# Attention, routing and two expert layers in one kernel: whole-chunk loads, masks before scans, two sets of one-hots, and the weight decoding's last steps inside the last expert

## The chip, the core and the metric

The kernel runs on one core of a Trainium2 chip. The metric is device time in microseconds (us); the time before is the median of three runs.

## The reference

The reference chains three stages. The first is a gated linear attention over 4 batches, 8 heads, 768 steps and a head width of 48. The second is a mixture of 8 experts with the two best per token, and the third a dense gated layer over all 3072 tokens.

```python
for t in range(S):
    state = alpha[:, :, t, :, None] * state + np.einsum('bhd,bhe->bhde', k[:, :, t], v[:, :, t])
    y[:, :, t] = np.einsum('bhd,bhde->bhe', q[:, :, t], state)
...
noisy_logits = x @ w_gate + np.log1p(np.exp(x @ w_noise)) * noise
top2 = np.argpartition(-noisy_logits, 2, axis=1)[:, :2]
...
h = np.maximum(x[mask] @ w1[e], 0.0)
out[mask] += top2_w[mask, k, None] * (h @ w2[e])
...
a = x @ w_a
b = x @ w_b
return (a * b @ w_out).astype(np.float32)
```

The weights of the third stage arrive as 64-bit floats; the kernel turns them into 32-bit floats on the chip.

## The kernel before, in words

The order of the work is written out by hand: each engine runs its instructions in the order in which the program issues them, and generators (`tick` for the routing, `bg` for the decoding) put side work between units of the main work. TensorE carries the main work.

**Attention.** Tokens go in 24 chunks of 128 (6 per batch). A chunk's q, k and alpha of all heads stand in one tile `ring[i % 6]` of 128 rows by 1536 columns: one head of each pair in rows 0 to 47, the other in rows 64 to 111. `load_qka` (L457) brings it. Chunks 0 to 5 come as full 128-row images from `qka0`, with zeros and ones in the 16 rows behind each half; later ones as two transfers of 48 rows from `qka1`, since the padding rows are then already in the tile. `prep(i)` (L496) runs two scans on VectorE (L503 into D, L507 into A) that make the products of decays, and GpSimd multiplies k and q by them (L505, L508, L511). The loop at L637 handles chunk i: it issues the loads of chunk i+5, then `prep(i+3)`, then transposes and gate inputs on TensorE, one `tick()`, the state's part of the output (`inter`, L549), the scores of chunk i+1 (`sc_unit`, L533) with the causal masks on VectorE (L538, into pm), then `intra` (L557), the gate products (L617), the state's update (`u_unit` L584, `s_unit` L599 and L600), each with further ticks. Scores use PSUM banks 2 and 3, so the scores of a chunk wait until the masks of the chunk before have read them.

**Routing.** `route(g)` (L216) is a generator for 14 and then 10 chunks; it ranks experts and places tokens with many small VectorE operations, partly on GpSimd. After the second group `lists()` (L356) makes the gather lists: for five chunks at a time VectorE writes one-hots `at` (L369), `eqk` (L369) and `bt` (L375), TensorE multiplies them into a list (L382) and VectorE adds it up (L383, into idx at the end). `at`, `eqk` and `bt` have one buffer each, and between making a set and multiplying it the generator yields four times. `weights()` (L386) follows.

**Experts.** Each expert has `up_unit`s (nine products per unit and column block, L682 to L684, read by L699 on ScalarE and L700 on VectorE; four PSUM banks in turn) and `down_unit`s (24 products). Gathers of the rows of the next expert go from GpSimd's queue (L415), and `x_unit` transposes them (L423, L425, L426). Expert 0 runs in two parts; behind the second part's up units the program flushes the routing (`while side: tick()`, L911) and issues the seven gathers of expert 1.

**Decoding.** `decode(c)` (L836) turns piece c of 36 of the 64-bit weights into floats in five steps, one per `bg()`: a load; ScalarE L845 and L846 with VectorE L847; VectorE L850 and L851; ScalarE L853 with GpSimd L854 and L855; VectorE L857 and a store. When expert 6 is done, `while decs: bg()` (L954) issues all steps that are left, ahead of expert 7's first up unit, so that the pool `dec` can be released and the tile EX take its place.

Of the kernel before, what the change touches and what calls it, by code (L numbers as in the profile page):

```python
# [8 lines left out]
F32R = mybir.dt.float32r  # L9
# [11 lines left out]
NT = B * NCH  # L21
# [39 lines left out]
@with_exitstack  # L61
def moe_kernel(ctx: ExitStack, tc, qka0, qka1, afirst, v, wgn, noise, w1, w2, w3, out):
    nc = tc.nc
# [10 lines left out]
    def bank(i):  # L74
        return tl(psum, [128, 512], F32, f"bank{i}")
# [78 lines left out]
    rows = sctx.enter_context(tc.tile_pool(name="rows", bufs=7))  # L154
    rt = sctx.enter_context(tc.tile_pool(name="rt", bufs=1))

# [59 lines left out]
    def route(g):  # L216
# [90 lines left out]
        if half:  # L307
# [3 lines left out]
            else:  # L311
# [10 lines left out]
        yield  # L322
        eq, bt = (tl(rt, [128, HOT, 2, E * NJ], F16, x).rearrange("p a k w -> p (a k w)")[:, :n * NJ]
                  .rearrange("p (a w) -> p a w", a=n) for x in ("eqk", "bt"))
# [7 lines left out]
        for j0 in range(0, n, m):  # L332
            at = tl(rt, [128, HOT, 2, 128], F16, "at").rearrange("p a k w -> p (a k) w")[:, :m]
            nc.vector.tensor_tensor(at, lane[:, None, :].to_broadcast([128, m, 128]),
                                    pf[:, j0:j0 + m, None].to_broadcast([128, m, 128]), op=ALU.is_equal)
            for _ in range(LAG):
                yield
            pl = spot(1, NJ)
            for j in range(m):
                nc.tensor.matmul(pl, at[:, j], bt[:, j0 + j], start=j == 0, stop=j == m - 1)  # L340
            acc = lacc[:, mine]
            nc.vector.tensor_tensor(idx0[:, mine] if j0 + m == n else acc, pl[:, mine], acc, op=ALU.add)
# [13 lines left out]
    def lists():  # L356

        pi, ki, pf, kf = (tl(rt, [128, NT, 2], dt, x) for x, dt in (("ei", I32), ("ri", I32), ("rf", F32), ("e1", F32)))
        nc.vector.tensor_scalar(pi, slot, 127, None, op0=ALU.bitwise_and)
        nc.vector.tensor_scalar(ki, slot, 7, None, op0=ALU.logical_shift_right)  # L360
        nc.vector.tensor_copy(pf, pi)
        nc.vector.tensor_copy(kf, ki)
        for j0 in range(0, NT, HOT):
            m = min(HOT, NT - j0)
            js = slice(j0, j0 + m)
            at, eq, bt = (tl(rt, [128, HOT, 2, w_], F16, x) for x, w_ in (("at", 128), ("eqk", E * NJ), ("bt", E * NJ)))
            for out_, src, val in ((at, lane, pf), (eq, keys, kf)):
                w_ = src.shape[-1]
                nc.vector.tensor_tensor(out_[:, :m].rearrange("p a k w -> p (a k) w"),  # L369
                                        src[:, None, :].to_broadcast([128, 2 * m, w_]),  # L370
                                        val[:, js].rearrange("p a k -> p (a k)")[:, :, None]
                                        .to_broadcast([128, 2 * m, w_]), op=ALU.is_equal)
                yield
            for k in range(2):
                nc.vector.tensor_tensor(bt[:, :m, k], eq[:, :m, k],  # L375
                                        token[:, js, None].to_broadcast([128, m, E * NJ]), op=ALU.mult)
            for _ in range(LAG + 1):
                yield
            pl = spot(1, E * NJ)
            for j in range(m):  # L380
                for k in range(2):
                    nc.tensor.matmul(pl, at[:, j, k], bt[:, j, k], start=j + k == 0, stop=j == m - 1 and k == 1)  # L382
            nc.vector.tensor_tensor(idx if j0 + m == NT else lacc, pl, lacc, op=ALU.add)  # L383
        yield
# [62 lines left out]
    with ExitStack() as actx:  # L447
# [9 lines left out]
        def load_qka(i):  # L457

            t = ring[i % RING]
            if i < 2:  # L460
                for c in (slice(1024, 1536), slice(512, 1024), slice(0, 512)):
                    nc.sync.dma_start(t[:, c], qka0[i, :, c])
            elif i < RING:
                nc.sync.dma_start(t[:, :1536], qka0[i])
            else:
                for h in range(2):
                    nc.sync.dma_start(t[64 * h:64 * h + 48, :1536], qka1[i - RING, 48 * h:48 * h + 48])

# [168 lines left out]
        for i in range(NT):  # L637
            if i + 5 < NT:
                load_qka(i + 5)
                load_v(i + 5)  # L640
            if i + 3 < NT:
                prep(i + 3)
            if i + 1 < NT:
# [5 lines left out]
            if i + 1 < NT:  # L649
                sc_unit(i + 1)  # L650
            else:
                x_unit(0, 0, bank(2))
                x_unit(0, 1, bank(3))
            tick()
            intra(i)
# [255 lines left out]
    while side:  # L911
        tick()
    for q in range(NJ):
        gather(1, q)
# [13 lines left out]
    for e in range(1, E - 1):  # L928
# [14 lines left out]
        for j in range(NJ):  # L943
# [9 lines left out]
            bg()  # L953
    while decs:  # L954
        bg()
    dec.release()
    epool = sctx.enter_context(tc.tile_pool(name="epool", bufs=1))
    EX = tl(epool, [128, (NF2 - 2) * 768], F32R, "EX")
    e = E - 1
    for f in range(NF1):  # L960
# [5 lines left out]
        if f >= NF1 - 4:  # L966
            load_more()
    tail = up_tail(e)
    next(tail)
# [177 lines left out]
```

## Time and profile before

| | us |
|---|---|
| median of 3 runs | 1097.96 |
| lowest, highest run | 1096.56, 1103.16 |
| the profiled execution | 1102.63 |
| its span on the core | 1100.8 |

The profile is of one execution, 4.7 us above the median. Its span leaves 1.8 us around it, and its mean granted TensorE clock is 0.984 of full speed. Times within it count from the span's start. In a row of the timeline stand the start, the time that the group took, engine, line, operation, operands and count; in brackets the engine's idle time before it and what ended that.

### The profile page before, as it was taken

What the parts mean: (1) busy time and instruction counts of PE and PEld (TensorE: products, weight loads), DVE (VectorE), ACT (ScalarE), POOL (GpSimd) and SP (SyncE); (2) the same over time, 40 slices, a digit from 0 to 9 for tenths busy, and PEclk for the clock granted to TensorE, in tenths of its full rate; (3) what the DMA queues carried; (4) which work ended last, traced back from release to release, by engine and by line L of the source; (5) the groups of instructions that cost most, each with busy time, mean ns of one, the idle gap of its engine ahead of it and who ended that gap; (6) DMA issues with size and microseconds to landing.
All of it is one profiled execution on the core that took longest, in us unless ns stands there. A gap on an engine that the chain in (4) does not pass through costs nothing.

```text
span 1100.8 us, 19103 instructions
## 1 busy us (share of the span) xinstructions
PE 1060.8 (96%) x7504; PEld 1026.1 (93%) x7504; DVE 467.2 (42%) x860; ACT 421.1 (38%) x929; POOL 405.4 (37%) x437
## 2 busy tenths in 40 slices
PE   7999899799999999999989999999999999999997
PEld 5888779799999999999978999999999999999997
DVE  8867846553342535353521453232323141414130
ACT  2435342354444555455542553222323232313131
POOL 5657631484654757575752553010101010100000
PEclk9989899999999999999998999999999999999999
DMA  8998322363544545544532552010101111010000
GB/s 284 217 199 192 97 73 83 111 217 100 168 134 140 163 155 171 173 162 152 176 122 79 165 164 70 22 44 22 37 29 29 37 30 37 22 37 1 22 1 24
DMA packets 59330, 114.57 MB, mean 104 GB/s; under 512 B 8144, under 2 KB 43776, under 8 KB 59232
## 3 DMA queue, kind: packets, MB, share of 16 engines
q1 hardware_dynamic: 52688, 93.49, 28.9%
q0 software_dynamic: 6544, 19.77, 6.0%
q8 instruction: 63, 1.03, 0.4%
q14 instruction: 35, 0.29, 0.1%
HBM read 86.38 MB, written 26.84 MB: 103 GB/s over the span
## 4 chain that ended last, share of the span: by engine, by line
PE 87%; DVE 5%; issue 3%; POOL 2%; ACT 1%; DMA 1%; another core or an unknown queue 0%; SPq 0%; POOLq 0%; ACTq 0%; DVEq 0%
PE bank L682 25%; PE bank L684 25%; PE bank L683 25%; PE bank L423 2%; PE bank L533 2%; PE bank L557 2%; PE bank L549 1%; PE bank L525 1%; PE bank L584 1%; DVE D L503 1%; DVE pm L538 1%; DVE A L507 1%; PE bank L494 1%; DMA wst<-w3f 1%; POOL rf L855 1%
## 5 line engine op out<-in xcount | busy, mean ns | idle before, releaser
L682 PE MATMUL bank<-X,W 128*128 128x384 f32 (+2 forms) x768 | 261.0, 340 | 4.6 <-DVE HB L700 3.9
L683 PE MATMUL bank<-X,W 128*128 128x384 f32 (+2 forms) x768 | 259.6, 338 | 0.6 <-DVE X L426 0.6
L684 PE MATMUL bank<-X,W 128*128 128x384 f32 (+2 forms) x768 | 259.6, 338 | 0.0
L114 POOL TENSOR_TENSOR W<-wst,W 128x384 fp32r<-128x384 f32 x136 | 139.0, 1028 | 145.4 <-ACT W L113 133.9
L880 POOL DMA_INDIRECT row<-y,row x48 | 46.3, 964 | 295.1 <-DVE row L888 186.2
L682 PEld LDWEIGHTS bank<-X,W 128*128 128x128 f32 x768 | 145.5, 189 | 7.7 <-DVE HB L700 4.6
L683 PEld LDWEIGHTS bank<-X,W 128*128 128x128 f32 x768 | 145.6, 190 | 2.8 <-DVE X L426 0.9
L684 PEld LDWEIGHTS bank<-X,W 128*128 128x128 f32 x768 | 145.3, 189 | 2.2
L682 PE MATMUL bank<-W,HB 128*128 128x384 f32 x416 | 145.6, 350 | 0.1
L684 PE MATMUL bank<-W,HB 128*128 128x384 f32 x416 | 140.9, 339 | 0.0
L683 PE MATMUL bank<-W,HB 128*128 128x384 f32 x416 | 140.7, 338 | 0.0
L1000 DVE TENSOR_TENSOR p<-bank,a 128x384 f32<-128x384 f32 x96 | 53.5, 557 | 166.7 <-PE bank L684 166.4
L426 DVE TENSOR_TENSOR X<-bank,X 128x384 fp32r<-128x384 f32 (+1 forms) x80 | 42.8, 538 | 182.7 <-ACT X L425 181.0
L1001 ACT ACTIVATE HB<-p 128x384 fp32r<-128x384 f32 x96 | 50.5, 526 | 155.7 <-DVE p L1000 152.1
L700 DVE SCALAR_TENSOR_TENSOR HB<-bank,HB 128x384 fp32r<-128x384 f32 (+2 forms) x128 | 71.2, 563 | 88.5 <-ACT HB L699 78.4
L699 ACT ACTIVATE HB<-bank 128x384 fp32r<-128x384 f32 (+2 forms) x128 | 63.4, 497 | 94.7 <-PE bank L684 82.1
L682 PE MATMUL bank<-EX,HB 128*128 128x384 f32 x240 | 82.1, 342 | 0.0
L683 PE MATMUL bank<-EX,HB 128*128 128x384 f32 x240 | 80.4, 335 | 0.0
L684 PE MATMUL bank<-EX,HB 128*128 128x384 f32 x240 | 80.3, 335 | 0.0
L682 PEld LDWEIGHTS bank<-W,HB 128*128 128x128 f32 x416 | 78.1, 188 | 0.8 <-ACT HB L699 0.4
L683 PEld LDWEIGHTS bank<-W,HB 128*128 128x128 f32 x416 | 78.3, 188 | 0.1
L684 PEld LDWEIGHTS bank<-W,HB 128*128 128x128 f32 x416 | 78.0, 188 | 0.2 <-DVE HB L700 0.2
(217 smaller groups left out, 1792.8 us busy)
## 6 DMA issues: line engine op xcount, KB each, us to landing
wst<-w SPq DMA_DIRECT2D x128, 192.0 KB
wd<-w SPq DMA_DIRECT2D x36, 384.0 KB
ring<-qka SPq DMA_DIRECT2D x36, 288.0 KB
y<-o SPq DMA_DIRECT2D x49, 192.0 KB
w3f<-u SPq DMA_DIRECT2D x36, 192.0 KB
wst<-w3f SPq DMA_DIRECT2D x36, 192.0 KB
v<-v SPq DMA_DIRECT2D x12, 384.0 KB
xd<-x SPq DMA_DIRECT2D x12, 384.0 KB
```

Source lines behind the costliest of these rows:

```text
L114: eng.tensor_tensor(l, raw, h.bitcast(F32), op=ALU.subtract)
L423: nc.tensor.transpose(pt[:, k * 128:k * 128 + m], t[:m, k * 128:k * 128 + 128], ident[:m, :m])
L426: nc.vector.tensor_tensor(l, ptv, h.bitcast(F32), op=ALU.subtract)
L533: nc.tensor.matmul(pb[h][:, p * 128:p * 128 + 128], part(i, h, NP + p), part(i, h, p), start=True, stop=True)
L682: nc.tensor.matmul(ps, ah, bh, start=first, stop=False)
L683: nc.tensor.matmul(ps, ah, bl, start=False, stop=False)
L684: nc.tensor.matmul(ps, al, bh, start=False, stop=last)
L699: nc.scalar.activation(Hh[:, f, s], pu, AF.Relu)
L700: nc.vector.scalar_tensor_tensor(Hl[:, f, s], pu, 0.0, Hh[:, f, s].bitcast(F32), op0=ALU.max, op1=ALU.subtract)
L880: nc.gpsimd.indirect_dma_start(out=t, out_offset=None, in_=src, in_offset=bass.IndirectOffsetOnAxis(ap=row[:, i, k:k + 1], axis=0))
L1000: nc.vector.tensor_tensor(p, ps[1], a, op=ALU.mult)
L1001: nc.scalar.activation(Ph[:, f], p, AF.Copy)
```

## The change

- **Loads.** The host pads all 24 chunks to 128 rows, in one array `qka`. From chunk 2 on each chunk is one transfer of 128 rows by 1536; the two transfers of 48 rows are gone (18 chunks, 18 fewer issues, 196,608 bytes more per chunk).
- **Masks ahead of scans.** `prep(i + 3)` moves in the loop from behind the loads to behind the scores of chunk i+1, so its scans stand behind that chunk's masks on VectorE.
- **One-hots.** `at`, `eqk` and `bt` have two buffers. `lists()` makes set j+1 before it multiplies set j, and yields three times per set where it yielded six times. The pool `rt` is taken from the other side of SBUF and released behind the flush of the routing.
- **Last decoding steps.** The up units of expert 7 each end with a `bg()`; the flush of the decoding, the release of `dec` and the allocation of EX stand behind them.

```diff
-            elif i < RING:
-                nc.sync.dma_start(t[:, :1536], qka0[i])
             else:
-                for h in range(2):
-                    nc.sync.dma_start(t[64 * h:64 * h + 48, :1536], qka1[i - RING, 48 * h:48 * h + 48])
+                nc.sync.dma_start(t[:, :1536], qka[i])
...
-            if i + 3 < NT:
-                prep(i + 3)
             if i + 1 < NT:
                 t_unit(i + 1)
...
                 x_unit(0, 1, bank(3))
+            if i + 3 < NT:
+                prep(i + 3)
             tick()
             intra(i)
...
+        yield from make(0)
+        for j0 in range(0, NT, HOT):
+            if j0 + HOT < NT:
+                yield from make(j0 + HOT)
+            else:
+                for _ in range(LAG):
+                    yield
+            m, at, bt = hot.pop(j0)
             pl = spot(1, E * NJ)
             for j in range(m):
                 for k in range(2):
                     nc.tensor.matmul(pl, at[:, j, k], bt[:, j, k], start=j + k == 0, stop=j == m - 1 and k == 1)
+            yield
             nc.vector.tensor_tensor(idx if j0 + m == NT else lacc, pl, lacc, op=ALU.add)
...
-    while decs:
-        bg()
-    dec.release()
-    epool = sctx.enter_context(tc.tile_pool(name="epool", bufs=1))
-    EX = tl(epool, [128, (NF2 - 2) * 768], F32R, "EX")
     e = E - 1
     for f in range(NF1):
         up_unit(e, f, [(0, CAPA)])
...
             load_more()
+        bg()
+    while decs:
+        bg()
+    dec.release()
+    epool = sctx.enter_context(tc.tile_pool(name="epool", bufs=1))
+    EX = tl(epool, [128, (NF2 - 2) * 768], F32R, "EX")
```

`make(j0)` holds the one-hot instructions of a set, unchanged, with the new buffers and two yields.

VectorE at the head of the attention loop, before; D and A are the scans, pm the masks, ss the state's update:

```order
L503 SCALAR_TENSOR_TENSOR D_235<-ring_35_129,bank_30_124 128x512
L506 RECIPROCAL bank_31_125<-D_235 128x4
L507 SCALAR_TENSOR_TENSOR A_236<-ring_35_129,bank_31_125 128x512
L503 SCALAR_TENSOR_TENSOR D_245<-ring_36_130,bank_30_124 128x512
L506 RECIPROCAL bank_31_125<-D_245 128x4
L507 SCALAR_TENSOR_TENSOR A_246<-ring_36_130,bank_31_125 128x512
L538 TENSOR_TENSOR pm_71_272<-bank_69_262,causal_72 128x512
L538 TENSOR_TENSOR pm_72_274<-bank_70_263,causal_72 128x512
L599 TENSOR_TENSOR ss_305<-bank_29_117,sc_233 128x192
```

The same place on VectorE now (L503 is L512, L538 is L547, L599 is L608):

```order
L512 SCALAR_TENSOR_TENSOR D_235<-ring_35_129,bank_30_124 128x512
L515 RECIPROCAL bank_31_125<-D_235 128x4
L516 SCALAR_TENSOR_TENSOR A_236<-ring_35_129,bank_31_125 128x512
L547 TENSOR_TENSOR pm_68_263<-bank_66_253,causal_72 128x512
L547 TENSOR_TENSOR pm_69_265<-bank_67_254,causal_72 128x512
L512 SCALAR_TENSOR_TENSOR D_267<-ring_36_130,bank_30_124 128x512
L515 RECIPROCAL bank_31_125<-D_267 128x4
L516 SCALAR_TENSOR_TENSOR A_268<-ring_36_130,bank_31_125 128x512
L608 TENSOR_TENSOR ss_305<-bank_29_117,sc_233 128x192
```

The two masks moved ahead of the scans of chunk 3; ss stands behind them as before.

VectorE in `lists()`, before; at, eqk and bt are a set of one-hots, lacc the sum, X and HB the main work's results:

```order
L369 TENSOR_TENSOR at_2491<-lane_108,rf_2485 128x1280
L369 TENSOR_TENSOR eqk_2492<-keys_107,e_500_2486 128x560
L375 TENSOR_TENSOR bt_2493<-eqk_2492,token_109 128x5x56 x2
L383 TENSOR_TENSOR lacc_110<-bank_508_2542,lacc_110 128x56
L369 TENSOR_TENSOR at_2554<-lane_108,rf_2485 128x1280
L369 TENSOR_TENSOR eqk_2555<-keys_107,e_500_2486 128x560
L375 TENSOR_TENSOR bt_2556<-eqk_2555,token_109 128x5x56 x2
L426 TENSOR_TENSOR X_96<-bank_514_2583,X_96 128x3x128
L426 TENSOR_TENSOR X_96<-bank_515_2595,X_96 128x3x128
L426 TENSOR_TENSOR X_96<-bank_516_2607,X_96 128x3x128
L383 TENSOR_TENSOR lacc_110<-bank_517_2619,lacc_110 128x56
```

The same place on VectorE now (L369 is L372, L375 is L378, L383 is L395, L426 is L438):

```order
L372 TENSOR_TENSOR at_2473<-lane_108,rf_2467 128x1280
L372 TENSOR_TENSOR eqk_2474<-keys_107,e_500_2468 128x560
L378 TENSOR_TENSOR bt_2475<-eqk_2474,token_109 128x5x56 x2
L372 TENSOR_TENSOR at_2496<-lane_108,rf_2467 128x1280
L372 TENSOR_TENSOR eqk_2497<-keys_107,e_500_2468 128x560
L378 TENSOR_TENSOR bt_2498<-eqk_2497,token_109 128x5x56 x2
L395 TENSOR_TENSOR lacc_110<-bank_509_2515,lacc_110 128x56
L372 TENSOR_TENSOR at_2537<-lane_108,rf_2467 128x1280
L372 TENSOR_TENSOR eqk_2538<-keys_107,e_500_2468 128x560
L378 TENSOR_TENSOR bt_2539<-eqk_2538,token_109 128x5x56 x2
L395 TENSOR_TENSOR lacc_110<-bank_515_2556,lacc_110 128x56
L372 TENSOR_TENSOR at_2574<-lane_108,rf_2467 128x1280
```

Set 2 stands ahead of the first sum, and three sets are made before the first X. On TensorE three of the five groups of list products stand ahead of the up units of expert 0's second part, where two stood, and the last two stand inside its first up unit and behind its second.

VectorE at the start of the last expert, before; u, pw and rf are the decoding, HB the last expert's up units:

```order
L857 SCALAR_TENSOR_TENSOR u_6816<-wd_6733,rf_6819 128x384
L847 TENSOR_SCALAR u_6914<-wd_6863 128x384
L850 SCALAR_TENSOR_TENSOR u_6914<-ah_6916,u_6914 128x384
L851 TENSOR_SCALAR pw_6915<-u_6914 128x384
L857 SCALAR_TENSOR_TENSOR u_6914<-wd_6863,rf_6917 128x384
L700 SCALAR_TENSOR_TENSOR HB_2270<-bank_1142_6933,HB_2270 128x512
L700 SCALAR_TENSOR_TENSOR HB_2270<-bank_1144_6949,HB_2270 128x512
L700 SCALAR_TENSOR_TENSOR HB_2270<-bank_1146_6965,HB_2270 128x512
L700 SCALAR_TENSOR_TENSOR HB_2270<-bank_1148_6991,HB_2270 128x512
```

The same place on VectorE now (L700 is L709, L847 is L856, L850 is L859, L857 is L866):

```order
L709 SCALAR_TENSOR_TENSOR HB_2252<-bank_1137_6895,HB_2252 128x512
L866 SCALAR_TENSOR_TENSOR u_6799<-wd_6716,rf_6802 128x384
L856 TENSOR_SCALAR u_6913<-wd_6846 128x384
L709 SCALAR_TENSOR_TENSOR HB_2252<-bank_1143_6920,HB_2252 128x512
L859 SCALAR_TENSOR_TENSOR u_6913<-ah_6915,u_6913 128x384
L860 TENSOR_SCALAR pw_6914<-u_6913 128x384
L709 SCALAR_TENSOR_TENSOR HB_2252<-bank_1145_6938,HB_2252 128x512
L709 SCALAR_TENSOR_TENSOR HB_2252<-bank_1147_6967,HB_2252 128x512
L866 SCALAR_TENSOR_TENSOR u_6913<-wd_6846,rf_6916 128x384
```

The five decoding operations, which stood in one run ahead of all the evictions, stand between the first five of them.

## Rows read from the trace of the kernel before

**Rows 1.** The page: busy time of the engines, and TensorE's granted clock in 40 slices.
```profile
PE 1060.8 (96%) x7504; PEld 1026.1 (93%) x7504; DVE 467.2 (42%) x860; ACT 421.1 (38%) x929; POOL 405.4 (37%) x437
...
PEclk9989899999999999999998999999999999999999
```

**Rows 2.** Busy time by stretch: length; PE, PEld, DVE, ACT, POOL; clock; DMA share; GB/s.
```profile
8.00:18.00 10.00, 8.77 (x112) 6.16 (x112) 7.16 (x11) 2.15 (x5) 4.35 (x5) 1.00 1.04 413
30.00:50.00 20.00, 19.88 (x379) 18.30 (x378) 18.06 (x26) 8.70 (x20) 13.28 (x15) 1.00 0.91 209
51.00:53.00 2.00, 0.37 (x16) 0.25 (x12) 0.29 (x1) 0.94 (x3) 0.69 (x2) 1.00 0.96 177
...
113.00:123.00 10.00, 8.80 (x92) 8.47 (x92) 9.69 (x19) 2.71 (x6) 6.90 (x10) 0.51 0.48 109
...
576.90:583.70 6.80, 5.69 (x13) 4.46 (x14) 3.54 (x6) 1.76 (x4) 3.61 (x5) 0.50 0.66 201
```

**Rows 3.** Timeline of TensorE in attention: the four longest waits.
```profile
20.89 1.66 PE L533 MATMUL bank<-ring 48*128 48x128 f32 x16 [1.54 <-DVE pm L538]
...
52.93 0.29 PE L584 MATMUL bank<-v,kn 128*48 128x48 f32 x4 [1.63 <-issue]
...
79.21 0.79 PE L533 MATMUL bank<-ring 48*128 48x128 f32 x2 [2.32 <-issue]
...
114.20 2.58 PE L533 MATMUL bank<-ring 48*128 48x128 f32 x16 [3.23 <-DVE pm L538]
```

**Rows 4.** Timeline of VectorE in attention: at the start, and with the first routing group.
```profile
17.50 1.19 DVE L503 TENSOR_TENSOR_SCAN D<-ring,bank 128x512 f32<-128x512 f32 x1
...
20.08 1.26 DVE L538 TENSOR_TENSOR pm<-bank,causal 128x512 f32<-128x512 f32 x2
...
103.89 1.26 DVE L538 TENSOR_TENSOR pm<-bank,causal 128x512 f32<-128x512 f32 x2
...
105.67 1.23 DVE L269 TENSOR_TENSOR r_eq<-r_eq,prio 128x112 f32<-128x112 f32 x1
...
113.38 1.28 DVE L538 TENSOR_TENSOR pm<-bank,causal 128x512 f32<-128x512 f32 x2
114.57 0.26 DVE L269 TENSOR_TENSOR r_eq<-r_eq,prio 128x112 f32<-128x112 f32 x1
```

**Rows 5.** Timeline of TensorE at the end of expert 0: list products, first gathered row.
```profile
200.14 0.19 PE L382 MATMUL bank<-bt,at 128*128 128x56 f16 x1 [0.86 <-DVE bt L375]
201.25 0.39 PE L382 MATMUL bank<-bt,at 128*128 128x56 f16 x7 [0.92 <-DVE bt L375]
...
213.04 0.55 PE L423 MATMUL bank<-ident,row 128*128 128x128 f32 x3 [2.95 <-DMA row<-xd,idx]
```

**Rows 6.** Timeline of ScalarE, VectorE and GpSimd, end of expert 0.
```profile
189.59 0.49 ACT L699 ACTIVATE HB<-bank 128x384 fp32r<-128x384 f32 x1 [1.38 <-PE bank L684]
191.15 0.49 ACT L699 ACTIVATE HB<-bank 128x384 fp32r<-128x384 f32 x1 [1.07 <-PE bank L684]
...
206.43 0.49 ACT L699 ACTIVATE HB<-bank 128x384 fp32r<-128x384 f32 x1 [1.11 <-PE bank L684]
...
205.72 0.17 DVE L399 TENSOR_SCALAR sm<-dm 128x24 f32<-128x24 f32 x1
...
206.62 0.54 DVE L850 SCALAR_TENSOR_TENSOR u<-ah,u 128x384 f32<-128x384 f32 x1
...
209.95 0.98 POOL L415 DMA_INDIRECT row<-xd,idx  x1
```

**Rows 7.** Timeline of TensorE and ScalarE at the start of the last expert.
```profile
573.71 0.39 PE L683 MATMUL bank<-X,W 128*128 128x512 f32 x1
573.94 0.39 PE L684 MATMUL bank<-X,W 128*128 128x512 f32 x1
578.01 0.79 PE L682 MATMUL bank<-X,W 128*128 128x512 f32 x1 [3.69 <-DVE HB L700]
...
589.13 0.60 ACT L699 ACTIVATE HB<-bank 128x512 fp32r<-128x512 f32 x1 [1.03 <-PE bank L684]
```

More of the change, by code (lines that the diff above doesn't have):

```diff
@@ L61, in moe_kernel @@
 @with_exitstack
-def moe_kernel(ctx: ExitStack, tc, qka0, qka1, afirst, v, wgn, noise, w1, w2, w3, out):
+def moe_kernel(ctx: ExitStack, tc, qka, afirst, v, wgn, noise, w1, w2, w3, out):
     nc = tc.nc
@@ L154, in moe_kernel @@
     rows = sctx.enter_context(tc.tile_pool(name="rows", bufs=7))
-    rt = sctx.enter_context(tc.tile_pool(name="rt", bufs=1))
+    rt = tc.alloc_tile_pool(name="rt", bufs=1, side="right")
     trn = [0]
@@ L322, in route @@
         yield
-        eq, bt = (tl(rt, [128, HOT, 2, E * NJ], F16, x).rearrange("p a k w -> p (a k w)")[:, :n * NJ]
+        eq, bt = (tl(rt, [128, HOT, 2, E * NJ], F16, x, bufs=2).rearrange("p a k w -> p (a k w)")[:, :n * NJ]
                   .rearrange("p (a w) -> p a w", a=n) for x in ("eqk", "bt"))
@@ L332, in route @@
         for j0 in range(0, n, m):
-            at = tl(rt, [128, HOT, 2, 128], F16, "at").rearrange("p a k w -> p (a k) w")[:, :m]
+            at = tl(rt, [128, HOT, 2, 128], F16, "at", bufs=2).rearrange("p a k w -> p (a k) w")[:, :m]
             nc.vector.tensor_tensor(at, lane[:, None, :].to_broadcast([128, m, 128]),
@@ L362, in lists, with make @@
         nc.vector.tensor_copy(kf, ki)
-        for j0 in range(0, NT, HOT):
+        hot = {}
+        def make(j0):
             m = min(HOT, NT - j0)
             js = slice(j0, j0 + m)
-            at, eq, bt = (tl(rt, [128, HOT, 2, w_], F16, x) for x, w_ in (("at", 128), ("eqk", E * NJ), ("bt", E * NJ)))
+            at, eq, bt = (tl(rt, [128, HOT, 2, w_], F16, x, bufs=2)
+                          for x, w_ in (("at", 128), ("eqk", E * NJ), ("bt", E * NJ)))
             for out_, src, val in ((at, lane, pf), (eq, keys, kf)):
@@ L376, in lists @@
                                         token[:, js, None].to_broadcast([128, m, E * NJ]), op=ALU.mult)
-            for _ in range(LAG + 1):
-                yield
+            hot[j0] = m, at, bt
+        yield from make(0)
[6 more added lines that the diff above has]
+            m, at, bt = hot.pop(j0)
             pl = spot(1, E * NJ)
@@ L461, in load_qka @@
                 for c in (slice(1024, 1536), slice(512, 1024), slice(0, 512)):
-                    nc.sync.dma_start(t[:, c], qka0[i, :, c])
-            elif i < RING:
-                nc.sync.dma_start(t[:, :1536], qka0[i])
-            else:
-                for h in range(2):
-                    nc.sync.dma_start(t[64 * h:64 * h + 48, :1536], qka1[i - RING, 48 * h:48 * h + 48])
+                    nc.sync.dma_start(t[:, c], qka[i, :, c])
+            else:
+                nc.sync.dma_start(t[:, :1536], qka[i])
         vts, aends = {}, {}
@@ L912, in moe_kernel @@
         tick()
+    rt.release()
     for q in range(NJ):
@@ L1118 @@
     t = np.concatenate(t, axis=3)
-    pad = np.concatenate([np.zeros((RING, 2, 16, 1024), np.float32), np.ones((RING, 2, 16, 512), np.float32)], axis=3)
+    pad = np.concatenate([np.zeros((NT, 2, 16, 1024), np.float32), np.ones((NT, 2, 16, 512), np.float32)], axis=3)
     pad[..., 1024::128] = 0
     arrays = {
-        "qka0": np.concatenate([t[:RING], pad], axis=2).reshape(RING, 128, 1536),
-        "qka1": t[RING:].reshape(NT - RING, 2 * D, 1536),
+        "qka": np.concatenate([t, pad], axis=2).reshape(NT, 128, 1536),
         "afirst": af,
```

## The prediction

> **What bounds the kernel now.** I read the page first. TensorE is busy for 96% of the span, and its granted clock reads 9 in most of the 40 slices [rows 1]. So another engine's work counts only where TensorE waits for it, or where such a wait pulls its clock down. The next view is the list of TensorE's waits and, at each one, the timeline. They lie in three places: the attention loop (the first 150 us), the end of expert 0 (190 to 213 us) and the start of expert 7 (574 us). All three are touched by the change.
>
> Each wait has to be read with the clock behind it. [...] In attention the clock is about half again from 113 to 123 us, behind the wait of 3.23 us [rows 2, 3]. [...]
>
> **Term 1, the last decoding steps.** Expert 7's first four up units run without a wait until 574.2 us. Then TensorE stands for 3.69 us, because the four banks are full and VectorE has not come to its first eviction [rows 7]. VectorE's order shows why: five decoding operations stand ahead of that eviction, and two of them need GpSimd's results. In the changed order each eviction stands ahead of its decoding operation, and four banks give about 8 us of room, so the stall goes. The gain follows from the spacing of the products: 573.94 - 573.71 = 0.23 us. The 36 products that are left (four units of nine) would take 36 x 0.23 = 8.3 us and end at 573.94 + 0.23 + 8.3 = 582.5 us; in fact the last one was read from 589.13 us on [rows 7]. That is 6.6 us, of which 3.69 are the wait and the rest the half clock.
>
> What could be late next is the splitting of expert 7's second weights on GpSimd, between whose steps the decoding now stands: eight splits and two decoding operations of about 1 us each have the 16 us of the up units to run in. That covers them; if the cover failed, one wait of a few us would come back. Bounds: 3.7 (the wait goes, a slow stretch comes anyway) to 7.1 (3.69 + 3.4). I take 6.6, since the spacing counts both together.
>
> **Term 2, the one-hots.** Before, VectorE makes a set, TensorE multiplies it, and only then can the next set be written. The last products wait 0.86 and 0.92 us for `bt` [rows 5]. Now every set is written one group ahead; there is no longer a point where TensorE arrives first. An up unit of this part takes 191.15 - 189.59 = 1.56 us, so seven more after the first take 10.9 us; in fact the last was read at 206.43, 16.8 us after the first [rows 6]. In the changed order two more groups of list products stand ahead of the first read, and one group stands behind it. A group takes about 0.3 us (an estimate from the 0.39 us of the last seven products [rows 5]). So the last unit ends at 189.6 + 0.6 + 10.9 + 0.3 = 201.4: 5.0 us earlier.
>
> Behind it stands the wait of 2.95 us for the first gathered row [rows 5]. The gather follows VectorE's L850 by 209.95 - 206.62 = 3.3 us [rows 6], since GpSimd's queue has the decoding of piece 1 ahead of it. This order is unchanged, so the wait stays and moves along with the units. Only the small operations of `weights()`, from L399 at 205.72 to L850 at 206.62 [rows 6], no longer stand ahead of L850; I count 0.8 us for them. Term 2 is 5.8 us. Bounds: 1.8 (the two waits alone) to 8.0 (the wait for the row goes too).
>
> **Term 3, masks ahead of scans.** At the start VectorE runs the scans of chunk 3 from 17.50 us on and the masks at 20.08, and TensorE waits 1.54 us for them [rows 3, 4]. Now the masks run at about 17.5, before TensorE is ready for the next scores (20.89 - 1.54 = 19.35). The wait goes; what is late next is the state's update, now behind both scans, so I keep 1.2 us. Bounds: 0 to 1.54.
>
> At the longer wait, 3.23 us at 114.20, I expect little. From the masks at 103.89 to those at 113.38 VectorE is never idle, and what it does in between is two scans and the routing's ranking operations [rows 4]. The new order has the same work between the same two masks; only which chunk the scans belong to differs. So I take nothing there, with bounds of -2 (a loss) to 8 (the wait and the slow stretch of 10 us go).
>
> **Term 4, padded loads.** From 8 to 18 us, where whole 128-row chunks arrive, the DMA moves 413 GB/s at a busy share of 1.04; from 30 to 50 us, with the halves, 209 GB/s at 0.91 [rows 2]. So a padded chunk (786,432 bytes) takes 1.9 us and the two halves (589,824 bytes) 2.8. No long wait on TensorE names a chunk's landing, so I count this at nothing. The cover is the distance: a chunk is loaded five ahead and scanned three ahead.
>
> [...]
>
> **The sum.** 6.6 + 5.8 + 1.2 = 13.6 us. The profiled execution took 1102.63 us, so it would take 1089. It lies 4.7 us above the median of 1097.96, about one wait with its slow stretch; I expect a median run after to be as much below its unlucky ones. So 1097.96 - 13.6 = 1084.4; I forecast 1084.
>
> **The rivals.**
>
> *The instruction waits go too.* Two of the waits in attention, 1.63 and 2.32 us, are named "issue" and stand in the middle of a line's row of products [rows 3], where no data can be missing; the DMA share there is near 1 (0.96 at 51 to 53 us [rows 2]). I read them as instructions that arrive late behind data. Faster chunk loads would shorten them. For it speaks the rate above; against it, that the total of bytes grows and that a padded chunk keeps every DMA engine for eight rows on end in place of three. If both go with slow stretches of 3.4 us each, 1.6 + 2.3 + 6.8 = 10.7 us go from the profiled execution: 1102.6 - 13.6 - 10.7 = 1078. With the wait at 114 us gone too, about 1070.
>
> *Ranking collides with GpSimd.* The same operation L269 takes 1.23 us at one place and 0.26 at the other [rows 4]. Now the ranking stands right behind the second scan, whose end starts GpSimd's multiplication of q. If some six operations each pay 1.0 us more, on a VectorE with no idle time, TensorE waits 6 us longer in the attention loop: 1084 + 6 = 1090. Against it: the collisions are there already in the old order.
>
> [...]
>
> *The padding costs DMA time.* If the rate stayed at 209 GB/s, the 18 x 196,608 = 3.54 MB more would be 17 us of transfer in a stretch that is already 0.91 busy. It decides from the point where a chunk lands after VectorE wants to scan it, two loop passes after its issue. Then TensorE waits chunk by chunk; with three more slow stretches (10 us) the time is 1084 + 17 + 10 = 1111, slower than before. Against it stands the 413 GB/s of whole chunks.
>
> **How the numbers follow.** A measurement of this kernel tells about 1% from no change, so faster means below 1087 and slower above 1109. The forecast has 0.50 (1081 to 1087, some of it just above). That the instruction waits go has 0.25 (1070 to 1081). The collisions, or a half of term 2, have 0.22 (1087 to 1097). The padding has 0.03. Faster comes from nearly all of the first and all of the second: 0.73; same is 0.24, slower 0.03. The range 1073 to 1090 leaves out the end of the second case and most of the far half of the third.
>
> **What would show it.** At the start of the last expert TensorE should have no wait above 0.5 us, and a granted clock of 1.00. No list product (now L393) should wait for `bt`, and the first transpose of a gathered row should come some 6 us earlier, still behind a wait of about 2. The first scores' wait of 1.54 us should be gone, and a wait of 2 to 3 us for pm should still stand in the pass of the first routing group. In the loop the DMA should move a chunk at near twice the rate. I am wrong if the terms 1 and 2 show but attention got longer, or if a new wait stands where an old one went.

## The result: 1088.9 us, a ratio of 0.9889 to before

| | before | after |
|---|---|---|
| median of 4 runs of each, on one chip (us) | 1097.26 | 1088.9 |
| lowest, highest (us) | 1096.47, 1103.16 | 1087.62, 1089.1 |
| ratio after to before, 95% interval | | 0.9889, 0.9858 to 0.9919 |
| the profiled execution, its span (us) | 1102.63, 1100.8 | 1087.62, 1085.8 |
| mean granted clock | 0.984 | 0.983 |

The time lies in the predicted range, 4.9 us above the forecast. The two medians of the table lie 0.8% apart, the ratio on record 1.1%; beside seven runs of the kernel before, the changed kernel gave 0.9889 again (experiments, last but one). The profiled span is 15.0 us shorter, more than the medians differ, since the profiled execution of before was the longest of its four. Where these 15.0 us come from shows at four marks on the same piece of work: the first up product after attention begins at 151.58 us before and at 151.92 now, the first transposed gathered row at 213.04 and 208.27, the first up product of the last expert at 565.98 and 559.29, the read of that expert's last up unit at 589.13 and 575.84. So attention as a whole gave nothing (+0.3). Up to the second mark 5.1 us went, by the one-hots; from there to the third 1.9; in the last expert's up units 6.6; and 1.7 behind them.

The 1.9 us are no wait. Between 260 and 540 us the products of the down units (bank<-W,HB) take 335 to 346 ns on average, before 338 to 349, and those of the up units 334 to 335 in both. The profile of the one-hots alone shows the same short products, those of the loads and of the decoding alone the long ones. So it belongs to the one-hots' part of the change; what in it does this (the pool `rt` on the other side of SBUF is one candidate) no run shows.

The page of the kernel after answers to [rows 1]:

```profile
PE 1053.0 (97%) x7504; PEld 1020.3 (94%) x7504; DVE 470.4 (43%) x860; ACT 420.9 (39%) x929; POOL 405.5 (37%) x437
...
PEclk9998699999999999999999999999999999999999
```

A slice is 27 us. Of the three 8s of before, those of the third slice and of the one at 580 us are gone; now the fourth and the fifth slice, 81 to 136 us, read 8 and 6. The stretches of the kernel after, in the columns of [rows 2]:

```profile
30.00:50.00 20.00, 19.88 (x405) 18.44 (x404) 18.07 (x26) 9.02 (x21) 12.87 (x16) 1.00 0.69 239
50.00:75.00 25.00, 24.87 (x464) 23.03 (x462) 21.96 (x33) 12.59 (x29) 18.15 (x21) 1.00 0.85 302
75.00:100.00 25.00, 21.45 (x417) 19.76 (x415) 21.37 (x32) 14.16 (x36) 20.98 (x28) 1.00 0.75 272
100.00:124.20 24.20, 18.24 (x183) 16.76 (x183) 18.31 (x36) 5.09 (x12) 12.03 (x14) 0.51 0.23 81
...
558.40:565.00 6.60, 6.60 (x33) 5.28 (x32) 1.05 (x2) 5.01 (x12) 4.83 (x5) 1.00 0.68 223
```

The chunk loads carry more (239 against 209 GB/s) at a lower busy share (0.69 against 0.91). Up to 100 us attention ran ahead of before: from 50 to 75 us TensorE does 464 products at full clock, before 402 at 0.86:

```profile
50.00:75.00 25.00, 23.25 (x402) 21.56 (x399) 17.54 (x26) 9.95 (x23) 14.50 (x18) 0.86 0.89 199
```

All of that lead is lost from 100 to 124 us, at 0.51 of the clock. TensorE's longest waits in attention say why (before: [rows 3]):

```profile
93.81 1.13 PE L558 MATMUL bank<-Sbd,ring 128*128 128x96 f32 x8 [1.00 <-ACT Sbd L582]
...
100.48 2.58 PE L542 MATMUL bank<-ring 48*128 48x128 f32 x16 [1.75 <-DVE pm L547]
...
111.12 0.60 PE L300 MATMUL bank<-xc,ones 128*128 128x8 f32 x2 [2.42 <-DVE ss L608]
...
120.81 0.83 PE L626 MATMUL bank<-wgn,gx 128*64 128x16 f32 x12 [2.50 <-DVE carry L313]
...
130.18 0.56 PE L593 MATMUL bank<-v,kn 128*48 128x48 f32 x16 [2.37 <-DVE lacc L342]
```

The 1.54 us at the start and the two issue waits (1.63, 2.32) are gone, and the wait for pm is 1.75 in place of 3.23. Three new waits of about 2.4 us stand behind it, for ss, carry and lacc. VectorE's order in these passes shows where they come from:

```profile
105.28 1.27 DVE L547 TENSOR_TENSOR pm<-bank,causal 128x512 f32<-128x512 f32 x2
106.47 1.20 DVE L512 TENSOR_TENSOR_SCAN D<-ring,bank 128x512 f32<-128x512 f32 x1
...
107.93 1.22 DVE L516 TENSOR_TENSOR_SCAN A<-ring,bank 128x512 f32<-128x512 f32 x1
...
109.34 1.48 DVE L291 TENSOR_TENSOR_SCAN xc<-d,oa 128x120 f32<-128x120 f32 x1
110.74 0.33 DVE L608 TENSOR_TENSOR ss<-bank,sc 128x192 f32<-128x192 f32 x1
116.47 1.29 DVE L547 TENSOR_TENSOR pm<-bank,causal 128x512 f32<-128x512 f32 x2 [5.40 <-PE bank L542]
...
119.14 1.22 DVE L516 TENSOR_TENSOR_SCAN A<-ring,bank 128x512 f32<-128x512 f32 x1
120.27 0.25 DVE L306 TENSOR_TENSOR r_rs<-bank,e 128x112 f32<-128x112 f32 x1
...
120.51 0.16 DVE L313 SCALAR_TENSOR_TENSOR carry<-bank,least 128x8 f32<-128x8 f32 x1
...
128.85 1.22 DVE L516 TENSOR_TENSOR_SCAN A<-ring,bank 128x512 f32<-128x512 f32 x1
129.99 0.14 DVE L342 TENSOR_TENSOR lacc<-bank,lacc 128x4 f32<-128x4 f32 x1
```

The state's products (L593), the gate products (L626) and the routing's sums (L300) all go into one PSUM bank (UG), and ss, carry and lacc are VectorE's reads of it, each 0.14 to 0.33 us long. TensorE's next products into the bank wait for these reads (the 2.42, 2.50 and 2.37 us above). In both orders the scans of a pass stand ahead of the reads. What changed is their place to the masks, for which TensorE must first have made the scores: at 116.47 us VectorE stood still for 5.40 us for them. Before, the scans ran ahead of the masks. Now two scans and a reciprocal (2.6 us) run between the masks and each of the reads. From the start of the masks to ss it is 5.46 us now; before it was 1.97:

```profile
118.24 1.26 DVE L538 TENSOR_TENSOR pm<-bank,causal 128x512 f32<-128x512 f32 x2
...
119.89 0.41 DVE L291 TENSOR_TENSOR_SCAN xc<-d,oa 128x120 f32<-128x120 f32 x1
120.21 0.33 DVE L599 TENSOR_TENSOR ss<-bank,sc 128x192 f32<-128x192 f32 x1
```

The rest of the difference is the routing's scan L291, which takes 1.48 us in place of 0.41. It now runs beside GpSimd's multiplication of q:

```profile
109.30 1.26 POOL L517 TENSOR_TENSOR ring<-ring,A 128x512 f32<-128x512 f32 x1 [0.22 <-DVE oa L288]
```

At the end of expert 0 no list product waits for `bt` (before: [rows 5]), and the wait for the row stays:

```profile
208.27 0.55 PE L435 MATMUL bank<-ident,row 128*128 128x128 f32 x3 [2.22 <-DMA row<-xd,idx]
```

In the last expert's up units TensorE has no wait for VectorE, and ScalarE's read of the last of them, at 589.13 in [rows 7], stands at

```profile
575.84 0.60 ACT L708 ACTIVATE HB<-bank 128x512 fp32r<-128x512 f32 x1 [1.03 <-PE bank L693]
```

### The profile page after: what moved, and what is told of

Read it like the earlier page. It is cut to its first block, busy times and chain, and to the rows that moved or that the text cites. A ratio compares the mean times of both kernels' runs of the same rounds, so it can differ in the third digit from the quotient of the medians.

```text
span 1085.8 us, 19031 instructions
## 1 busy us (share of the span) xinstructions
PE 1053.0 (97%) x7504; PEld 1020.3 (94%) x7504; DVE 470.4 (43%) x860; ACT 420.9 (39%) x929; POOL 405.5 (37%) x437
## 3 DMA queue, kind: packets, MB, share of 16 engines
q8 instruction: 63, 1.03, 0.4%
## 4 chain that ended last, share of the span: by engine, by line
PE 91%; DVE 4%; ACT 1%; issue 1%; DMA 1%; POOL 1%; another core or an unknown queue 0%; SPq 0%; POOLq 0%; ACTq 0%; DVEq 0%
PE bank L691 26%; PE bank L693 26%; PE bank L692 26%; PE bank L435 2%; PE bank L542 2%; PE bank L558 2%; PE bank L566 2%; DVE pm L547 1%; PE bank L534 1%; DVE A L516 1%; PE bank L593 1%; DVE D L512 1%; DMA wst<-w3f 1%; PE bank L615 1%; PE bank L626 0%
## 5 line engine op out<-in xcount | busy, mean ns | idle before, releaser
L438 DVE TENSOR_TENSOR X<-bank,X 128x384 fp32r<-128x384 f32 (+1 forms) x80 | 42.9, 538 | 180.8 <-ACT X L437 179.0
L709 DVE SCALAR_TENSOR_TENSOR HB<-bank,HB 128x384 fp32r<-128x384 f32 (+2 forms) x128 | 71.3, 563 | 85.8 <-ACT HB L708 76.0
```

The lines of the kernel that those rows point to most:

```text
L438: nc.vector.tensor_tensor(l, ptv, h.bitcast(F32), op=ALU.subtract)
L709: nc.vector.scalar_tensor_tensor(Hl[:, f, s], pu, 0.0, Hh[:, f, s].bitcast(F32), op0=ALU.max, op1=ALU.subtract)
```

## The experiments

Theory A: the scans that were moved gain at the start and lose more in the passes of the routing, by the three waits and the half clock behind them. Theory C: the padded loads earn what the scans lose, since the issue waits go with them; its form C1 says that a busy DMA is what makes instructions late. Ratios are to runs of the kernel before on the same chip; 0.01 is 11 us.

**All scans back ahead of the masks** (loop pass as before, all else changed):

```diff
             if i + 5 < NT:
                 load_qka(i + 5)
                 load_v(i + 5)
+            if i + 3 < NT:
+                prep(i + 3)
...
                 x_unit(0, 1, bank(3))
-            if i + 3 < NT:
-                prep(i + 3)
```

> The changed kernel with the scans at their old place, ahead of the masks; everything else as changed. Theory A (the moved scans stand ahead of VectorE operations that TensorE waits for in the passes of the first routing group: ss, carry, lacc): these waits of 2.4, 2.5 and 2.4 us shrink to under 1, the slow stretch from 100 to 124 us goes or halves, the wait of 1.5 us at the start comes back, and the time falls to 1077 to 1082. Theory B (the passes got slower because TensorE came to them faster, whatever the order): the waits stay, 1088 to 1091.

Measured: 1077.37 us, ratio 0.9777 (0.9721 to 0.9833). The waits of TensorE above 1.3 us in attention, in the timeline:

```profile
19.78 1.66 PE L542 MATMUL bank<-ring 48*128 48x128 f32 x16 [1.54 <-DVE pm L547]
...
103.57 2.58 PE L542 MATMUL bank<-ring 48*128 48x128 f32 x16 [3.40 <-DVE pm L547]
```

The wait at the start is back, the one for pm is 3.40 again, and ss, carry and lacc cost 0.9 us at most. From the masks to carry it is 1.45 us, 2.6 less than in the changed kernel (116.47 to 120.51):

```profile
113.66 1.29 DVE L547 TENSOR_TENSOR pm<-bank,causal 128x512 f32<-128x512 f32 x2 [1.14 <-PE bank L542]
...
115.11 0.16 DVE L313 SCALAR_TENSOR_TENSOR carry<-bank,least 128x8 f32<-128x8 f32 x1
```

Without its second part the change is some 12 us better.

**The scans alone behind the masks** (the kernel before with that one move):

```diff
-            if i + 3 < NT:
-                prep(i + 3)
             if i + 1 < NT:
                 t_unit(i + 1)
...
                 x_unit(0, 1, bank(3))
+            if i + 3 < NT:
+                prep(i + 3)
```

> The kernel before with the moved scans alone. Theory A: the start is 1.2 us shorter, the passes of the first routing group 8 to 12 us longer, 1102 to 1109. Theory B: 1095 to 1098.

Measured: 1111.67 us, ratio 1.0094 (1.0057 to 1.0131), over the 1109 us expected; on this chip the kernel before took 1102.18. The three waits in its timeline:

```profile
117.38 0.59 PE L300 MATMUL bank<-xc,ones 128*128 128x8 f32 x2 [2.42 <-DVE ss L599]
127.07 0.83 PE L617 MATMUL bank<-wgn,gx 128*64 128x16 f32 x12 [2.50 <-DVE carry L313]
136.88 0.56 PE L584 MATMUL bank<-v,kn 128*48 128x48 f32 x16 [2.38 <-DVE lacc L342]
```

They are the same to 0.01 us, at other times. Taken alone, the move costs about 10 us; with the run above, it is shown from both sides that the move makes these waits and the loss.

**Halves again** (the changed kernel with two transfers of 48 rows per chunk) and **the padded loads alone** (the kernel before with one transfer of 128 rows):

```diff
-                nc.sync.dma_start(t[:, :1536], qka[i])
+                for h in range(2):
+                    nc.sync.dma_start(t[64 * h:64 * h + 48, :1536], qka1[i - RING, 48 * h:48 * h + 48])
```

> The changed kernel with the loads of before (two transfers of 48 rows from chunk 6 on). Theory C (the halves hold up TensorE's instructions): waits named issue of 1.5 to 2.5 us come back between 40 and 90 us, with slow stretches behind them, and the time is 1093 to 1099. Theory D (these waits in the profile of before were chance): none comes back, 1088 to 1090.

> The kernel before with the padded loads alone. Theory C: no issue wait over 0.6 us from 40 to 90 us, 1087 to 1092. Theory D: 1096 to 1098, as the kernel before.

Measured: with halves 1099.39 us, ratio 0.9985 (0.9957 to 1.0013); the loads alone 1092.03, ratio 0.9904 (0.9872 to 0.9937). TensorE's waits with halves:

```profile
52.82 0.29 PE L596 MATMUL bank<-v,kn 128*48 128x48 f32 x4 [1.98 <-issue]
76.05 0.48 PE L545 MATMUL bank<-ring 48*128 48x128 f32 x2 [2.07 <-issue]
85.51 0.83 PE L629 MATMUL bank<-wgn,gx 128*64 128x16 f32 x12 [3.25 <-issue]
```

The first two stand at the places of [rows 3], behind the same number of products of the line (4 and 2 are left). With the loads alone no issue wait above 0.3 us stands between 22 and 110 us; one of 1.09 us stands at 133.13. The loads are worth between 10 and 11 us either way: theory C. They also narrow the scatter: the eight runs of the loads alone lie within 3.8 us, the ten with halves within 11.1, and 23 of the kernel before on this chip within 14.4.

**Two transfers of 64 rows** for the same padded chunk, in the changed kernel:

```diff
-                nc.sync.dma_start(t[:, :1536], qka[i])
+                for h in range(2):
+                    nc.sync.dma_start(t[64 * h:64 * h + 64, :1536], qka[i, 64 * h:64 * h + 64])
```

> The changed kernel with each padded chunk from 6 on as two transfers of 64 rows: the bytes of the changed kernel, the form of the halves. Theory C1 (a transfer to one half of the partitions is slow, whatever its bytes): the rate in the loop falls to near 210 GB/s, issue waits of 1.5 us and more come back between 40 and 90 us, 1096 to 1106. Theory C2 (the 48-row form was slow because of its number of rows, not because of the half): the rate stays near 300 GB/s, no such wait, 1087 to 1091.

Measured: 1102.37 us, ratio 1.001 (0.9977 to 1.0042). Its stretch from 30 to 50 us, and two of its waits:

```profile
30.00:50.00 20.00, 19.24 (x384) 17.63 (x383) 17.03 (x25) 8.05 (x18) 13.03 (x16) 1.00 0.99 247
```

```profile
52.82 0.29 PE L596 MATMUL bank<-v,kn 128*48 128x48 f32 x4 [2.25 <-issue]
...
107.49 0.24 PE L596 MATMUL bank<-v,kn 128*48 128x48 f32 x1 [3.03 <-issue]
```

Two more issue waits stand in it, 0.99 us at 89.58 and 1.41 us at 98.35, though the profiled execution, 1093.73 us, was the fastest of the ten. The bytes and the rate are those of the whole transfer (247 and 239 GB/s), the share is 0.99 in place of 0.69, and by the median the gain is gone. So in these runs neither the bytes nor the padding mattered, but how many rows one transfer covers (ratios of 0.9985 with 48, 1.001 with 64 and 0.9889 with 128). The rate that was expected to fall did not: the kernel asks for so much, and the share is what it takes.

**More traffic in whole transfers** (all scans back, and behind each chunk from chunk 6 on a further load of 128 rows by 768 into a tile that nothing reads):

```diff
                 nc.sync.dma_start(t[:, :1536], qka[i])
+                if i >= RING:
+                    nc.sync.dma_start(tl(big, [128, 768], F32, "more", bufs=1), qka[i, :, :768])
```

> The changed kernel with all scans back ahead of the masks, and with a further load of 128 rows by 768 (393,216 bytes) behind each chunk from chunk 6 on, into a tile that nothing reads. The chunks stay single transfers of 128 rows, but the DMA share from 30 to 50 us should go from 0.70 to about 1. Theory C1 (the issue waits are instructions that come late behind a busy DMA, whatever its shape): one to three issue waits of 1.4 us or more come back between 40 and 110 us at the places in the instruction stream where they stood before, and the ratio to the kernel before goes from 0.978 to 0.984 to 0.992. Rival (what counts is that a transfer over half of the partitions keeps some of the DMA engines busy at one time, so whole transfers leave gaps whatever their sum): no issue wait above 1 us, and a ratio of 0.976 to 0.980.

Measured: 1078.37 us, ratio 0.98 (0.9757 to 0.9842). Its stretches:

```profile
30.00:50.00 20.00, 19.87 (x375) 18.29 (x375) 18.07 (x26) 8.83 (x20) 13.22 (x15) 1.00 0.89 304
50.00:75.00 25.00, 24.83 (x496) 23.06 (x492) 20.54 (x31) 12.47 (x29) 17.01 (x20) 1.00 0.92 329
75.00:100.00 25.00, 21.65 (x372) 19.72 (x371) 17.99 (x29) 13.14 (x35) 20.39 (x28) 1.00 0.92 317
```

The share is about that of the halves (0.91 in [rows 2]), half as many bytes again move, there are two issues per chunk as with halves, and no issue wait stands between 22 and 110 us. C1 in its plain form falls: a share of 0.89 to 0.92 alone brought no issue wait. The issue waits came with transfers over half of the rows (0.99 to 3.25 us in the two runs above). The rival's outcome came, its reason did not show: with such transfers the mean share of the 16 DMA engines is 0.91 [rows 2] and 0.99, so nearly all of them were busy.

**The one-hots alone** (`lists()`, its buffers and the pool `rt` as in the change's diff) and **the decoding steps alone** (below), each in the kernel before:

```diff
-    while decs:
-        bg()
-    dec.release()
...
         if f >= NF1 - 4:
             load_more()
+        bg()
+    while decs:
+        bg()
+    dec.release()
```

> The kernel before with the doubled one-hots alone. Term 2: the first gathered row of expert 1 is transposed 5 to 6 us earlier and the time is 5 to 6 us (0.5%) under the kernel before. Rival: later waits take it back, within 1 us of before.

> The kernel before with the last decoding steps inside the last expert alone. Term 1: no wait at the start of expert 7, no slow stretch there, 6 to 7 us (0.6%) under the kernel before. Rival: the splits of its second weights become late behind the decoding and a wait of 3 us or more stands at its first down unit, under 3 us gained.

Measured: the one-hots 1090.67 us, ratio 0.9921 (0.9888 to 0.9954), some 8.7 us; the decoding 1094.84, ratio 0.9938 (0.9908 to 0.9968), some 6.8. The first is over its expectation, but its interval reaches down to 5. In its profile the first gathered row is transposed 56.34 us after the first up product, where it was 61.46 before: 5.1 us, as expected. The short down products give 1.8 us more up to the last expert. In the second's profile the last expert's last up unit is read 369.69 us after the first gathered row, where it was 376.09 before: 6.4 us.

**Scans at the end of the pass**, behind the state's update:

```diff
-            if i + 3 < NT:
-                prep(i + 3)
             tick()
             intra(i)
...
                 s_unit(i + 1)
+            if i + 3 < NT:
+                prep(i + 3)
```

> The changed kernel with the scans later still: behind the state's update at the end of a pass, so that ss and most of the routing's operations stand ahead of them, as the masks do. Theory A (what counts is what stands ahead of an operation that TensorE waits for): the waits for ss, carry and lacc fall under 1 us each, the start has no wait for masks, and the time is 1071 to 1079. Theory A2 (scans must be done early in a pass, and any later place makes GpSimd and the state late): new waits for ring or Sbd of a us per pass, over 1088.

Measured: 1080.23 us, ratio 0.982 (0.9774 to 0.9866). Waits in its timeline:

```profile
98.46 0.82 PE L534 MATMUL bank<-ident,ring 128*128 128x128 f32 x4 [1.81 <-POOL ring L514]
101.93 2.58 PE L542 MATMUL bank<-ring 48*128 48x128 f32 x16 [2.01 <-DVE pm L547]
134.63 0.57 PE L558 MATMUL bank<-Sbd,ring 128*128 128x96 f32 x3 [2.53 <-ACT Sbd L582]
```

The waits for ss and carry are under 0.8 us and the one for lacc is 0.93, as theory A has it. But the time is 1.2 us above A's range, for the scans' own readers (GpSimd's L514 on the ring) are now late: the new waits for ring and Sbd that A2 named stand there, once each and not in every pass. The change gains no more than with the scans in their old place.

**Only the start's scans behind the masks**, and beside it on the same chip **the changed kernel again**, unaltered:

```diff
-            if i + 3 < NT:
+            if i == 0:
                 prep(i + 3)
```

with `if 0 < i < NT - 3: prep(i + 3)` ahead of `t_unit(i + 1)` for the other passes.

> The changed kernel with the scans of chunk 3 alone behind the masks (loop pass 0) and those of all later chunks ahead of them, as they were. Main theory (the moved scans gain only at the start, and lose in the passes of the routing groups, where ss, the routing's sum and its list stand behind them): no wait of 1.54 us at the start and no slow stretch behind it, no waits for ss, carry and lacc above 1 us, the wait of about 3 us for pm in the first routing pass still there; 1.5 to 4 us less than with all scans back, that is a ratio to the kernel before of 0.974 to 0.977. Rival (the start's gain is lost later, because TensorE then waits for a chunk's load or for the routing instead): a wait of 1.5 us or more somewhere before 100 us that the version with all scans back does not have, and the ratio stays at 0.978.

> The changed kernel itself, beside the other two on the same chip. Main theory: a ratio to the kernel before of 0.987 to 0.991, which is 11 to 15 us above the version with only the start's scans moved, with the waits of 2.4 us for ss, 2.5 for carry and 2.4 for lacc and half clock from about 100 to 124 us. Rival (the difference between the versions came from the chips that they ran on): less than 6 us between them here.

Measured: 1076.58 us, ratio 0.9789 (0.9747 to 0.9831), and 1087.47, ratio 0.9889 (0.9846 to 0.9932). The changed kernel's time and its waits came again; the difference of 10.9 us is not one of chips. In the first one's profile the wait at the start is gone, and one wait above 1.3 us is left in attention:

```profile
101.68 2.58 PE L542 MATMUL bank<-ring 48*128 48x128 f32 x16 [3.41 <-DVE pm L547]
```

Its span is 2.0 us shorter than with all scans back (1073.7 and 1075.7), but over all runs the two cannot be told apart (0.9789 and 0.9777): the start's gain is in the trace, not in the median. The expected 0.974 to 0.977 did not come; nor did the rival's wait ahead of 100 us.

**One pass more:** the same, with the scans of chunk 20 at the end of loop pass 17.

```diff
-            if 0 < i < NT - 3:
+            if 0 < i < NT - 3 and i != 17:
                 prep(i + 3)
...
                 s_unit(i + 1)
+            if i == 17:
+                prep(i + 3)
```

> The version with the start's scans alone behind the masks, and in addition the scans of chunk 20 (loop pass 17, the pass in which TensorE waits 3.41 us for pm) moved from the head of that pass to its end. Theory V (that wait is a matter of order: 2.6 us of scans and 1.6 us of ranking stand ahead of two masks on VectorE): the wait for pm of pass 17 falls to 0.5 to 1.5 us and the stretch of half clock behind it goes; 3 to 6 us less, a ratio to the kernel before of 0.973 to 0.976. Rival W (VectorE is simply full here, 21.8 of the 25 us from 75 to 100, and 20.9 of the next 25: whatever is put off is waited for in the next pass, where now four scans stand ahead of the masks): the wait for pm is as long one pass later, with its slow stretch, and the ratio stays at 0.978 to 0.982.

Measured: 1078.65 us, ratio 0.9771 (0.973 to 0.9812). The wait for pm is gone altogether (V), and one of 4.94 us stands in the next pass (W):

```profile
108.57 0.59 PE L300 MATMUL bank<-xc,ones 128*128 128x8 f32 x2 [4.94 <-DVE ss L608]
```

Ahead of that ss VectorE runs four scans on end, from 99.97 us, the masks at 105.16 and the routing's scan. Both were half right: the order decides which wait it is, and VectorE, busy for 21.72 of the 25 us from 75 to 100 and for 20.03 of the next 25, had no room for the work put off. The ratio lies between the two expectations and is that of all scans back.

## Why the prediction was right, and where it was not

The direction and the range came true, and two of the four terms. By the prediction's own line (faster means below 1087 us) 1088.9 us is not yet faster, and it lies in the stretch to which 0.22 was given; the ratio of 0.9889 has 1% inside its interval. The other two terms were each wrong by over 10 us, in opposite directions. That they nearly cancel is luck, and the forecast stands on it.

| | predicted, us | measured alone, us |
|---|---|---|
| last decoding steps | 6.6 gain | 6.8 gain |
| one-hots | 5.8 gain | 8.7 gain (in its profile 5.1 up to the gathered row, 1.8 in the down products) |
| masks ahead of scans | 1.2 gain | 10.3 loss |
| padded loads | 0 | 10.6 gain |
| sum | 13.6 gain | 15.8 gain; the whole change 12.2 |

The right column is the ratios' distance from 1 by 1100 us; each carries some 3 to 4 us of uncertainty, so the sum and the whole agree.

**Term 1** was right with its mechanism: no wait, a clock of 1.00 from 558.40 to 565.00 us, and 6.6 us between the marks of the last expert's up units. GpSimd's splits kept their cover: from 559 to 620 us no wait of TensorE names them.

**Term 2** was right. The eight up units of expert 0's second part take 11.24 us from the first read (191.20) to the last (202.44), where 10.9 was worked out and 16.84 stood before. The wait for the gathered row stayed, at 2.22 us. The shorter down products of the experts are a gain that the term did not have.

**Term 3** failed at one step: "The new order has the same work between the same two masks; only which chunk the scans belong to differs." The sentence is true and the wrong question. It asks when the masks run, and TensorE waits for other results of VectorE too: ss, carry and lacc. They come as soon behind the masks as VectorE can bring them, and now the scans stand between, so that each comes 2.6 us later behind its masks. The prediction had named the state's update as late next, for the start, and did not carry it to the passes of the routing, where VectorE works without a gap from 98 to 111 us. Its "wait of 2 to 3 us for pm should still stand" was wrong too: it fell to 1.75. The lower bound of -2 was far too narrow, since a wait was priced without what follows it: the clock was half for 24 us on end. At the start the step held: the 1.54 us went.

**Term 4** failed at "I count this at nothing". The cover held (no chunk was late). Of the rate, "near twice" did not come: it went from 209 to 239 GB/s, since the kernel asks for no more (with more traffic 304 came), and it is the share that fell, to 0.69. What it left to a rival with 0.25 was the side effect on the instructions. That rival gave 10.7 us for two waits and their slow stretches, and the loads alone measure 10.6. The 3.4 us that it and the bounds of term 1 count for a slow stretch are half of 6.8: in the trace of before the clock is 0.50 for 6.8 us at each of these two waits (from 54.6 and 78.5 us on) as at the start of expert 7 [rows 2]. The rival's reading was right in part: the waits are tied to the loads, but by their shape and not by the share of busy DMA that it pointed to.

**The ranking rival** (0.22, 1090 us) ends near the measured time, but mostly by another mechanism. L269, its example, takes 1.23 us once and 0.25 once, as before. Three other operations became slow with the move: L273 takes 1.05 us in place of 0.28, L291 1.48 in place of 0.41 and L317 1.22 in place of 0.16. All three run beside GpSimd's multiplication of q, as the rival had it, and with the scans back they are short again (0.27, 0.41, 0.17). That makes 2.9 us, of which only the 1.07 of L291 stand between masks and one of the three reads. Between the masks and carry or lacc (waits of 2.50 and 2.37 us) no operation is slower than before. So the larger part of the loss is order, and the smaller these long operations. That GpSimd makes them long no run shows, only that they run beside it. **The padding rival** is refuted by the share of 0.69.

**The sum** against the median held: the execution profiled after is 1.3 us below its median, the one before was 5 above.

The best version that was run is the changed kernel with its scans back in their old place, or with the start's scans alone moved: 0.978, twice the gain of the change. These two cannot be told apart here.

## What to carry to other kernels

When long work on an in-order engine is moved behind an instruction that waits for another engine, it no longer fills that wait, and everything behind it comes later by its whole length: here by 2.6 us, and TensorE waited 2.37 to 2.50 us for three results. So list the results behind it that other engines wait for, small reads of a shared PSUM bank above all, and price each. A time that comes out as forecast proves no term: run the parts alone, since two of four here were wrong by the size of the whole effect. Where TensorE waits in the middle of a line's row of products for "issue", look at the shape of the transfers that run beside it: here such waits of 1.0 to 3.3 us stood beside transfers over half of the rows, and none above 0.3 us (22 to 110 us) beside whole ones.

## What the runs showed of the hardware that was not expected

- From 30 to 50 us the same padded chunks took a DMA share of 0.69 as one transfer of 128 rows and 0.99 as two of 64, at 239 and 247 GB/s. Why, no run shows.
- Beside transfers over half of the rows stood waits of 1.0 to 3.3 us for issue. Beside whole ones, at a share of up to 0.92, none above 0.3 us stood between 22 and 110 us. The places recur in the stream of instructions: before and with halves the waits stand behind 719 and 1092 products of TensorE, the third one with halves behind 1217, those with two of 64 behind 719, 1341, 1466 and 1592. These lie 124 to 126 products apart, or a multiple of that. The page lists a queue "instruction" with 63 packets and 1.03 MB, 16 KB each, in the kernel after as before. In the trace of before the two waits end 1.50 and 1.29 us after a packet of this queue has landed (at 51.43 and 77.92 us), and the second packet starts late: at 76.83 us, when all 1092 earlier products have begun, while in the kernel after it starts at 66.09 us, with 87 products still to go. The places and the packets make it likely that TensorE waits there for what this queue brings, but no run took its packets away, and why the shape of the data transfers makes them late stays open.
- The half clock behind a wait differed a lot in length. Behind the wait of 3.40 us for pm, with all scans back, it lasts 6.8 us:

```profile
103.40:110.20 6.80, 6.63 (x81) 6.31 (x82) 6.56 (x16) 1.62 (x4) 4.23 (x6) 0.50 0.17 67
```

With the 4.94 us of the last run it lasts 13.5:

```profile
105.20:118.70 13.50, 10.13 (x98) 9.60 (x99) 9.86 (x26) 1.99 (x5) 8.10 (x10) 0.50 0.12 36
```

In the kernel after, where waits of 1.75, 2.42 and 2.50 us follow each other at some 10 us, it lasts 24 us on end (100.00:124.20 above). So these three waits cost far more than their 6.7 us: 24.2 us at 0.51 of the clock are worth about 12 (an estimate).
